# Light convolution and hard-swish feed-forward: block 0's exchange, last out bank and block 1's convolution put elsewhere in the order

## The chip, the cores and the metric

One core of one Trainium2 chip. The time is device microseconds of one execution of the program; the median of three runs is given. The engines are TensorE (PE, with its weight loads as PEld), VectorE (DVE), ScalarE (ACT), GpSimd (POOL), and SyncE (SP), which issues most DMAs.

## The reference

x is 8 sequences x 4096 tokens x 192 channels. The first part is a causal convolution of 7 taps, its weights a softmax for each of 8 groups of 24 channels; the second a feed-forward layer of width 2048 with a hard-swish gate. Cut to what matters:

```python
w = np.exp(weight - weight.max(-1, keepdims=True)); w = w / (w.sum(-1, keepdims=True) + 1e-9)
y[b, s, h, g] = sum(w[h, k] * x_pad[b, s + k, h, g] for k in range(7))      # 6 zeros ahead
h = y.reshape(32768, 192) @ w_in                                            # 192 x 2048
g = h * np.clip(h + 3.0, 0.0, 6.0) / 6.0
out = g @ w_out                                                             # 2048 x 192
```

x and the convolution's weight come as float32, w_in and w_out as 8-byte floats.

## The kernel before, in words

**Tiling.** 32768 tokens are 32 blocks of 1024, each two groups of 512. Channels lie on 64 partitions in three thirds; the lower 64 partitions hold one group of tokens, the upper 64 the other. `y` is the convolved block, [128, 3, 512]. It is split into a high part (ACT, L416) and a low part (DVE, L419), `y_own`, so that three passes of products (PASSES, L28) give the precision wanted. `y_other` is the same with the two halves of the partitions exchanged; the exchange is made by DMAs that SP issues (`swap`, L294 to L296).

**First layer.** A block has 16 units, each one of 8 pairs of columns of w_in for the own or the other half: 18 matmuls (L433) into one of four slots of two PSUM banks, then a relu on ACT (L307) and the gate on DVE (L311) into `g`. Slots go round in `free_slots`: a unit pops the first and appends it behind its gate.

**Second layer.** From block 1 on it is a scheme of products of sums (L503 on). Block 0 does it directly instead: `direct_chunk` (L356, matmuls at L322) adds one eighth of the sum into out banks, three banks in all. The first two are the two banks of one slot, `taken`, which is set aside at the unit r == 2; they are filled among the units of the loop and after it. The third is filled after that. `direct_out` transposes a bank on DVE (L367) and stores it.

**Start.** The weights' 8-byte words are loaded and rounded on the way, in 16 "units" of `Rounding` (L162): w_in 0, w_in 1, then w_in and w_out in turn, at last three of w_out. A load is 384 KB, two DMAs for w_in (L143) and one for w_out (L151), all issued by SP. `split` is two instructions of DVE (L181, L185), `clamp` three of ACT (L193, L196, L199), `join` two of DVE (L202, L206) and one of POOL (L210), `part`, for w_in alone, one of ACT (L218) and two of POOL (L219, L220). Four stages are there for w_out.

Inside `manual_schedule` (L716) every engine does its instructions in the order of the program. Block 0's convolution comes first, by thirds (`conv_units`, and for a third and a part PE itself, L731); as soon as a third of y is ready its parts are exchanged by `high_y` and `low_y`. The last third to come is number 1. `thirds_of` makes the first products of units 0 and 8 from the thirds that are there. Then the loop over r (L812) goes through the units, own and other in turn: products, relu, the `part` of the weight before, `clamp`, `join`, some loads, the gate, a `split`, and from r == 5 on every second time a chunk of the direct second layer. Behind the loop come `prepare` (block 1's convolution, one multiply on ACT and six taps on DVE, and the split of y), two last chunks, `direct_out` of the two banks, eight chunks of the third bank, `begin_block_two` (sums of w_out, small sums on POOL, part of block 2's convolution), `direct_out` of the third bank, the exchange for block 1, and the loop over blocks 1 to 31.

Of the kernel before, what the change touches and what calls it, by code (L numbers as in the profile page):

```python
# [8 lines left out]
ALU = mybir.AluOpType  # L9
# [22 lines left out]
def kernel(  # L32
# [8 lines left out]
    nc = tc.nc  # L41
# [3 lines left out]
    H, KC = weight.shape  # L45
# [3 lines left out]
    N = 512  # L49
# [43 lines left out]
    for base, dma in ((0, nc.scalar), (D2, nc.sync)):  # L93
        dma.dma_start(  # L94
            out=w_sb[base : base + D2],
# [4 lines left out]
    x_tiles = {0: xs.tile([P, K3, PAD + N], F32, name="x")}  # L100
    nc.vector.memset(x_tiles[0][0:D2, :, 0:PAD], 0.0)

    def load_x0(s, dma_lower, dma_upper):
        head, lower, upper = x_source(0)
        dma_lower.dma_start(out=x_tiles[0][0:D2, s, head:], in_=lower[:, s])  # L105
        dma_upper.dma_start(out=x_tiles[0][D2:P, s, :], in_=upper[:, s])
# [55 lines left out]
    class Rounding:  # L162
# [10 lines left out]
        def load(self):  # L173
            self.st = self.load_words()

        def split(self, engine=nc.vector):
            high = self.st[:, :, 1]
            self.top = cnv.tile([P, WS], U32, name="top")
            self.scale = cnv.tile([P, WS], U32, name="scale")
            self.sig = cnv.tile([P, WS], F32, name="sig")  # L180
            engine.tensor_scalar(  # L181
                out=self.scale[:], in0=high, scalar1=0x7FF00000, scalar2=None,
                op0=ALU.bitwise_and,
            )
            engine.tensor_scalar(  # L185
                out=self.top[:], in0=high, scalar1=0xFFFFF, scalar2=0x100000,
                op0=ALU.bitwise_and, op1=ALU.bitwise_or,
            )

        def clamp(self):  # L190


            nc.scalar.activation(  # L193
                self.sig[:], self.scale[:], ACT.Relu, bias=bias_e[:, 0:1], scale=-1.0
            )
            nc.scalar.activation(  # L196
                self.scale[:], self.sig[:], ACT.Relu, bias=bias_e[:, 1:2], scale=-8.0
            )
            nc.scalar.mul(self.sig[:], self.st[:, :, 0], 2.0**-52)  # L199

        def join(self):
            nc.vector.scalar_tensor_tensor(  # L202
                out=self.scale[:], in0=self.st[:, :, 1], scalar=0x80000000,
                in1=self.scale[:], op0=ALU.bitwise_and, op1=ALU.bitwise_or,
            )
            nc.vector.scalar_tensor_tensor(  # L206
                out=self.sig[:], in0=self.top[:], scalar=2.0**-20, in1=self.sig[:],
                op0=ALU.mult, op1=ALU.add,
            )
            nc.gpsimd.tensor_tensor(  # L210
                out=self.sig[:] if len(self.dst) > 1 else self.dst[0],
                in0=self.sig[:], in1=self.scale[:].bitcast(F32), op=ALU.mult,
            )

        def part(self):
            if len(self.dst) > 1:
                high, low, full = self.dst
                nc.scalar.mul(r32(high), self.sig[:], CUT)  # L218
                nc.gpsimd.tensor_copy(out=r32(full), in_=self.sig[:])  # L219
                nc.gpsimd.tensor_tensor(  # L220
                    out=r32(low), in0=self.sig[:], in1=high, op=ALU.subtract
                )
# [8 lines left out]
    def w_out_unit(j):  # L231
        dst = w_out[:, j, B11 : B22 + 1].rearrange("p b d -> p (b d)")
        return Rounding(lambda: load_w_out(j), [dst])
# [10 lines left out]
    for j in range(2, NP):  # L244
        units += [w_in_unit(j), w_out_unit(j - 2)]
    units += [w_out_unit(j) for j in range(NP - 2, NP)]
    AHEAD = 4
    for n in range(AHEAD):
        units[n].load()
        if n == 0:  # L250
            load_x0(1, nc.sync, nc.sync)
# [5 lines left out]
        out=e_sb[:], in0=w_sb[:], in1=mx[:].to_broadcast([P, KC]), op=ALU.subtract  # L257
# [3 lines left out]
    c_sb = cst.tile([P, KC], F32, name="c_sb")  # L261
# [5 lines left out]
    y = ys.tile([P, K3, N], F32, name="y")  # L267
# [35 lines left out]
    psum = ps.tile([P, 2 * 4, N], F32, name="psum")  # L303
    free_slots = list(range(4))

    def relu(r6, h):
        nc.scalar.activation(r6, h, ACT.Relu, bias=half[:], scale=1.0 / 6.0)  # L307

    def gate(g_, h):

        nc.vector.scalar_tensor_tensor(  # L311
            out=g_, in0=g_, scalar=1.0, in1=h, op0=ALU.min, op1=ALU.mult
        )
# [113 lines left out]
    def products(n, slot, s, steps=range(3), begin=False, end=False):  # L427
        group, c = divmod(n, NP)
        for m_ in steps:
            wn, yn = PASSES[m_]  # L430
            for k in range(2):
                r = slice(k * D2, (k + 1) * D2)
                nc.tensor.matmul(  # L433
                    out=psum[:, 2 * slot + k], lhsT=r32(w_in_parts[wn][r, c, s]),
                    rhs=r32(y_other[r, yn, s] if group else y_own[yn][r, s]),
                    start=begin and m_ == 0, stop=end and m_ == 2, skip_group_check=True,
                )

    def places(n, slot):
        group, c = divmod(n, NP)  # L440
        return g4[:, c, 1:3] if group else g4[:, c, 0::3], psum[:, 2 * slot : 2 * slot + 2]
# [274 lines left out]
    with tc.manual_schedule():  # L716
# [4 lines left out]
            out=c_sb[:], in0=e_sb[:], in1=sm[:].to_broadcast([P, KC]), op=ALU.mult  # L721
# [15 lines left out]
        for _ in range(3):  # L737

            nc.tensor.matmul(
                out=psum[:, b], lhsT=zeros[:, 0:P], rhs=zeros, start=True, stop=True  # L740
# [10 lines left out]
        def thirds_of(n, which, end=False):  # L751
            if n not in early:
                early[n] = free_slots.pop(0)
            for m_ in range(3):
                for s in which:
                    products(
                        n, early[n], s, (m_,), s == pe_third, end and s == which[-1]
                    )
# [5 lines left out]
        def low_y(s, of):  # L764
            low_of(y_own[LOW][:, thirds[s]], of, y_own[HIGH][:, thirds[s]], nc.vector)
            swap(y_other[:, LOW, thirds[s]], y_own[LOW][:, thirds[s]])

        def all_of(s):
            return y[:, thirds[s]]
# [14 lines left out]
        low_y(pe_third, psum[:, b : b + 1])  # L784
        high_y(0, all_of(0))
        low_y(0, all_of(0))
        for n in range(AHEAD, 2 * AHEAD):
            load(n)
        thirds_of(0, (pe_third, 0))
        thirds_of(NP, (pe_third, 0))  # L790
        split(1)
# [5 lines left out]
        join(1)  # L797
        part(1)
        low_y(1, all_of(1))
        for n in (8, 9, 10, 12):  # L800
            load(n)
        split(2)
        clamp(2)
# [1 line left out]
        thirds_of(0, (1,), True)  # L805
        thirds_of(NP, (1,), True)

        joins = {0: 2, **{n - 1: n for n in range(3, len(units))}}
        loads = {3: 11, 5: 13, 7: 14, 9: 15}
        taken = None  # L810
        waiting = [1]
        for r in range(2 * NP):  # L812
            c, group = divmod(r, 2)
            k = c + group * NP
            if k in early:
                slot = early[k]
            else:
                slot = free_slots.pop(0)
                for m_ in range(3):
                    for s in range(K3):  # L820
                        products(k, slot, s, (m_,), s == 0, s == K3 - 1)
            to, both = places(k, slot)
            relu(to, both)
            n = joins.get(r)
            if r - 1 in joins:
                part(joins[r - 1])
            if n is not None:
                clamp(n + 1)
                join(n)
                if n in loads:  # L830
                    load(loads[n])
            gate(to, both)
            if r == 2:
                taken = slot
                banks = [(h, psum[:, 2 * slot + h]) for h in range(2)]
                x_tiles[1] = load_x(1)
            else:
                free_slots.append(slot)
            if n is not None:
                split(n + 2)  # L840
            if r >= 5 and r % 2:
                direct_chunk(banks, (r - 5) // 2)
        start_pools.close()

        def conv_jobs(i):
            x = x_tiles.pop(i)
            jobs = [lambda: nc.scalar.mul(y[:], x[:, :, 0:N], c_sb[:, 0:1])]  # L847
            for k in range(1, KC):
                jobs.append(lambda k=k: nc.vector.scalar_tensor_tensor(  # L849
                    out=y[:], in0=x[:, :, k : k + N], scalar=c_sb[:, k : k + 1], in1=y[:],  # L850
                    op0=ALU.mult, op1=ALU.add,
                ))
            return jobs

        def split_y():
            split_high()
            split_rest()
# [5 lines left out]
            low_of(y_own[LOW][:], y[:], y_own[HIGH][:], nc.vector)  # L863

        def prepare():
            for job in conv_jobs(1):
                job()
            x_tiles[2] = load_x(2, nc.gpsimd)
            split_y()
# [14 lines left out]
        for r, bank in banks:  # L884
            direct_out(0, r, bank)
        free_slots.append(taken)
        third = 2, psum[:, 2 * free_slots[0]]
        for p in every:
            direct_chunk([third], p)
        begin_block_two()  # L890
# [7 lines left out]
        for i in range(1, NB):  # L898
            jobs = {4 * n + 1: [job] for n, job in enumerate(conv[4:])}
# [47 lines left out]
```

## Time and profile before

| | us |
|---|---|
| median of three runs | 2234.03 (2233.31 to 2237.73) |
| the profiled execution's own time | 2237.14 |
| its span | 2235.0 |
| PE busy | 2216.5 (99%) |
| DVE busy | 1811.7 (81%) |
| ACT busy | 936.0 (42%) |
| POOL busy | 829.0 (37%) |
| start to block 1's first product | 108.23 |
| block 1's first layer, second layer | 35.70, 35.47 |
| block 2's first layer, second layer | 32.87, 35.47 |

The profile is of one execution; L12 is line 12 of the kernel. Busy PE is modelled from pipelined matmuls, and says nothing of the clock that PE was granted, which is a row of its own (1.00 is full). A wait names the instruction that waited, what released it, and the time that its engine was idle. The span leaves out some 2 us of the execution's own time.

### The profile page before, as it was taken

How to read it: one execution, taken by the hardware profiler on the slowest of the kernel's cores; microseconds unless marked ns; L12 is line 12 of the kernel's file. 1: busy time of each engine (PE TensorE's matmuls, PEld its weight loads, DVE VectorE, ACT ScalarE, POOL GpSimd, SP SyncE). 2: the span in 40 equal slices, each digit the busy share in tenths (PEclk: the TensorE clock that was granted, in tenths of full speed). 3: DMA queues.
4: the chain of work that ended last, by engine and by line, in shares of the span. 5: the costliest groups of instructions: out<-in, count | busy, mean ns of one | idle time of the engine just before them, and what ended most of it. 6: DMA issues, size and time to landing. Idle time of an engine off the chain costs nothing.

```text
span 2235.0 us, 49342 instructions
## 1 busy us (share of the span) xinstructions
PE 2216.5 (99%) x21598; PEld 1543.1 (69%) x21598; DVE 1811.7 (81%) x1588; ACT 936.0 (42%) x1172; POOL 829.0 (37%) x706
## 2 busy tenths in 40 slices
PE   8999999999999999999999999999999999999999
PEld 4477766777766777667777667776677776677766
DVE  7878888888887888888888888888888888888866
ACT  6444433444333444334443334443344433344433
POOL 3344322444223443224442234432244422344322
PEclk9999999999999999999999999999999999999999
DMA  6143233342233332333322333223333223332232
GB/s 163 36 91 58 43 68 76 63 77 34 58 76 70 70 55 44 69 76 63 76 34 58 77 70 70 54 44 71 75 65 77 34 58 76 70 70 53 41 61 34
DMA packets 249096, 142.91 MB, mean 64 GB/s; under 512 B 207121, under 2 KB 212241, under 8 KB 248881
## 3 DMA queue, kind: packets, MB, share of 16 engines
q1 hardware_dynamic: 230392, 105.86, 23.4%
q0 software_dynamic: 17248, 33.64, 8.7%
q8 instruction: 169, 2.77, 0.5%
q10 hardware_dynamic: 1240, 0.27, 0.1%
q14 instruction: 47, 0.38, 0.1%
HBM read 31.72 MB, written 25.17 MB: 25 GB/s over the span
## 4 chain that ended last, share of the span: by engine, by line
PE 97%; DVE 1%; DMA 1%; SPq 0%; ACT 0%; issue 0%; POOL 0%; DVEq 0%; ACTq 0%; POOLq 0%
PE psum L529 49%; PE psum L433 47%; PE psum L322 1%; DVE y L849 1%; DMA x<-in_x_dram 0%; DMA y_other<-y 0%; SPq L143 0%; ACT y L847 0%; DVE y L284 0%; SPq L295 0%; SPq L105 0%; SPq L296 0%; SPq L151 0%; DVE results L401 0%; SPq L94 0%
## 5 line engine op out<-in xcount | busy, mean ns | idle before, releaser
L529 PE MATMUL psum<-g,w_out 128*32 128x512 f32 (+1 forms) x6712 | 967.4, 552 | 0.0
L311 DVE SCALAR_TENSOR_TENSOR g<-g,psum 128x1024 f32<-128x1024 f32 x512 | 618.9, 1218 | 213.4 <-ACT g L307 213.1
L307 ACT ACTIVATE g<-psum,half 128x1024 f32<-128x1024 f32 x512 | 572.4, 1118 | 506.2 <-PE psum L433 478.1
L492 POOL TENSOR_TENSOR s<-g 128x256 f32<-128x256 f32 x248 | 268.7, 1084 | 1252.1 <-DVE g L311 957.2
L433 PE MATMUL psum<-y,w_in 64*128 64x512 f32 x4608 | 538.5, 391 | 3.0 <-DVE results L367 3.0
L529 PEld LDWEIGHTS psum<-g,w_out 128*32 128x32 f32 x6712 | 370.9, 110 | 246.9 <-issue 126.7
L433 PE MATMUL psum<-y_other,w_in 64*128 64x512 f32 x4608 | 530.8, 387 | 8.4 <-DMA y_other<-y 8.1
L433 PEld LDWEIGHTS psum<-y,w_in 64*128 64x128 f32 x4608 | 434.1, 186 | 122.1 <-issue 29.8
L433 PEld LDWEIGHTS psum<-y_other,w_in 64*128 64x128 f32 x4608 | 434.2, 184 | 99.0 <-DMA y_other<-y 10.4
L529 PE MATMUL psum<-s,w_out 128*32 128x512 f32 (+1 forms) x3272 | 465.4, 570 | 0.0
L849 DVE SCALAR_TENSOR_TENSOR y<-x,c_sb,y 128x1536 f32<-128x1536 f32 x186 | 334.9, 1800 | 2.8 <-ACT y L847 1.6
L381 POOL TENSOR_TENSOR s<-g 128x1024 f32<-128x1024 f32 x93 | 297.8, 3202 | 25.1 <-DVE g L311 25.1
L529 PE MATMUL psum<-g,w_s 128*32 128x256 f32 x1240 | 282.8, 379 | 0.0
L529 PEld LDWEIGHTS psum<-s,w_out 128*32 128x32 f32 x3272 | 153.8, 110 | 80.1 <-issue 48.4
L529 PEld LDWEIGHTS psum<-g,w_s 128*32 128x32 f32 x1240 | 136.4, 110 | 68.2
L381 DVE TENSOR_TENSOR s<-g 128x2048 f32<-128x2048 f32 (+1 forms) x93 | 177.2, 1934 | 1.1
L529 PE MATMUL psum<-s,w_s 128*32 128x256 f32 x744 | 170.7, 379 | 0.0
L492 DVE TENSOR_TENSOR g<-g 128x1024 f32<-128x1024 f32 x124 | 151.9, 1225 | 5.3
L381 DVE TENSOR_TENSOR g<-g 128x2048 f32<-128x2048 f32 x62 | 139.1, 2284 | 0.0
L401 DVE TENSOR_TENSOR p<-psum,p 32x256 f32<-32x256 f32 (+1 forms) x93 | 47.7, 513 | 96.5 <-PE psum L529 95.1
L401 DVE TENSOR_TENSOR results<-psum,results 32x256 f32<-32x256 f32 (+3 forms) x128 | 69.2, 541 | 51.0 <-issue 47.2
L526 ACT COPY psum<-psum 32x512 f32<-32x512 f32 x93 | 51.3, 551 | 135.4 <-PE psum L529 135.4
(88 smaller groups left out, 1092.1 us busy)
## 6 DMA issues: line engine op xcount, KB each, us to landing
y_other<-y SPq DMA_DIRECT2D x124, 384.0 KB, 5.0
g<-g POOLq DMA_DIRECT2D x62, 512.0 KB, 5.0
out_dram<-results SPq DMA_DIRECT2D x378, 64.0 KB, 2.0
x<-in_x_dram SPq DMA_DIRECT2D x53, 388.5 KB, 7.1
g<-in_moe_w_in_dram SPq DMA_DIRECT2D x16, 192.0 KB, 5.6
stage<-in_moe_w_out_dram SPq DMA_DIRECT2D x8, 384.0 KB, 3.9
x<-in_x_dram SPq DMA_DIRECT2D x7, 384.0 KB, 6.5
y_other<-y SPq DMA_DIRECT2D x12, 128.0 KB, 2.3
```

The source lines that it names most:

```text
L307: nc.scalar.activation(r6, h, ACT.Relu, bias=half[:], scale=1.0 / 6.0)
L311: nc.vector.scalar_tensor_tensor(out=g_, in0=g_, scalar=1.0, in1=h, op0=ALU.min, op1=ALU.mult)
L322: lambda p=p: nc.tensor.matmul(out=bank[j * QS : (j + 1) * QS, tokens], lhsT=w_out[:, p, w, cols], rhs=x[:, p, tokens], start=(first and p ...
L381: engine.tensor_tensor(out=o[:, r], in0=a[:, r], in1=b[:, r], op=op)
L401: nc.vector.tensor_tensor(out=out, in0=x, in1=y, op=op)
L433: nc.tensor.matmul(out=psum[:, 2 * slot + k], lhsT=r32(w_in_parts[wn][r, c, s]), rhs=r32(y_other[r, yn, s] if group else y_own[yn][r, s]), ...
L492: engine.tensor_tensor(out=o, in0=p, in1=q, op=op)
L526: streams[3].append((t - 0.5, lambda: fn(*args, **kw)))
L529: nc.tensor.matmul(out=out, lhsT=w, rhs=x, start=start, stop=True, tile_position=(0, j * QS), skip_group_check=True,)
L849: jobs.append(lambda k=k: nc.vector.scalar_tensor_tensor(out=y[:], in0=x[:, :, k : k + N], scalar=c_sb[:, k : k + 1], in1=y[:], op0=ALU.mu ...
```

## The change

It has three parts, all of them in block 0 or just behind it; the arithmetic is the same.

1. Three weight units instead of four are loaded at the start. Unit 3 is loaded behind the exchange of third 0, where units 4 to 7 were, and these are loaded behind the exchange of third 1, ahead of 8, 9, 10 and 12.
2. Block 1's convolution is taken apart: its multiply on ACT is issued at the end of r == 6 of the loop, one tap at the ends of r == 9, 11, 13 and 14, and the last two taps where all seven instructions were, in `prepare`.
3. The third out bank is a bank of the last slot in `free_slots`, not of the first.

```diff
-    AHEAD = 4
-    for n in range(AHEAD):
+    for n in range(3):
         units[n].load()
...
         low_y(0, all_of(0))
-        for n in range(AHEAD, 2 * AHEAD):
-            load(n)
+        load(3)
         thirds_of(0, (pe_third, 0))
         thirds_of(NP, (pe_third, 0))
...
         low_y(1, all_of(1))
-        for n in (8, 9, 10, 12):
+        for n in (4, 5, 6, 7, 8, 9, 10, 12):
             load(n)
...
+        conv1 = []
         joins = {0: 2, **{n - 1: n for n in range(3, len(units))}}
...
             if n is not None:
                 split(n + 2)
+            if r == 6:
+                conv1.extend(conv_jobs(1))
+                conv1.pop(0)()
+            if r in (9, 11, 13, 14):
+                conv1.pop(0)()
             if r >= 5 and r % 2:
                 direct_chunk(banks, (r - 5) // 2)
...
         def prepare():
-            for job in conv_jobs(1):
+            for job in conv1:
                 job()
             x_tiles[2] = load_x(2, nc.gpsimd)
             split_y()
...
         free_slots.append(taken)
-        third = 2, psum[:, 2 * free_slots[0]]
+        third = 2, psum[:, 2 * free_slots[-1]]
         for p in every:
             direct_chunk([third], p)
```

`conv_jobs` itself only moves ahead of the loop: it returns the multiply (L847) and the six taps (L849) as a list.

More of the change, by code (lines that the diff above doesn't have):

```diff
@@ L806, with conv_jobs @@
         thirds_of(NP, (1,), True)
+        def conv_jobs(i):
+            x = x_tiles.pop(i)
+            jobs = [lambda: nc.scalar.mul(y[:], x[:, :, 0:N], c_sb[:, 0:1])]
+            for k in range(1, KC):
+                jobs.append(lambda k=k: nc.vector.scalar_tensor_tensor(
+                    out=y[:], in0=x[:, :, k : k + N], scalar=c_sb[:, k : k + 1], in1=y[:],
+                    op0=ALU.mult, op1=ALU.add,
+                ))
+            return jobs
+        conv1 = []
         joins = {0: 2, **{n - 1: n for n in range(3, len(units))}}
@@ L843 @@
         start_pools.close()
[L845 to L853, printed above, removed]
         def split_y():
```

## The prediction

> **What bounds the kernel.** I read the page first, its chain that ended last:
>
> ```profile
> PE 97%; DVE 1%; DMA 1%; SPq 0%; ACT 0%; issue 0%; POOL 0%; DVEq 0%; ACTq 0%; POOLq 0%
> ```
>
> TensorE (PE) has 97% of the span, so only idle or slowed PE time is worth anything. Next all waits of PE (us in total, times, longest):
>
> ```profile
> PE psum L433 <- DMA y_other<-y: 8.1, 2, 7.3
> PE psum L433 <- DVE results L367: 3.0, 1, 3.0
> ```
>
> Besides 1.7 us at the very start that is all PE waits in 2235 us. Where they lie is in PE's timeline (start, duration, instruction, count, idle before), 16 to 46 us and behind 91 us:
>
> ```profile
> 21.04 0.85 PE L433 MATMUL psum<-y,w_in 64*128 64x512 f32 x6
> 29.20 2.16 PE L433 MATMUL psum<-y_other,w_in 64*128 64x512 f32 x6 [7.32 <-DMA y_other<-y]
> 31.16 4.04 PE L433 MATMUL psum<-y,w_in 64*128 64x512 f32 x18
> ...
> 107.38 0.71 DVE L367 STREAM_TRANSPOSE results<-psum 128x512 f32<-128x512 f32 x1
> ...
> 108.23 19.38 PE L433 MATMUL psum<-y,w_in 64*128 64x512 f32 x144 [3.04 <-DVE results L367]
> ```
>
> Both lie at block 0. The first product that needs the exchanged last third of y waits 7.32 us; block 1's first product waits 3.04 us until the third out bank is transposed out of the slot it takes first. Each wait costs more than itself. In the table of stages (columns: PE, PEld, DVE, ACT, POOL busy, granted clock, DMA share, GB/s)
>
> ```profile
> 18.53:21.95 3.42, 2.42 (x18) 1.34 (x16) 3.42 (x5) 1.61 (x4) 2.80 (x3) 1.00 0.84 219
> 103.87:107.28 3.41, 1.32 (x16) 0.13 (x4) 3.38 (x2) 0.00 (x0) 0.00 (x0) 1.00 0.09 13
> 107.28:110.69 3.41, 2.46 (x12) 2.16 (x14) 3.37 (x4) 0.00 (x0) 0.00 (x0) 0.50 0.38 61
> ```
>
> the granted clock falls to 0.50 at 107.3 us and is back at 114.1; around the other wait it is 0.50 from 25.4 to 35.6. 18 matmuls take 4.04 us at 31.16, and 2.2 at full clock. Block 1's first layer lasts 108.23 to 143.93 = 35.70 us, block 2's 32.87: 2.83 us of slow clock.
>
> Why the exchange is late is in SP's queue:
>
> ```profile
> 18.30 0.60 SPq L296 DMA_DIRECT2D y_other<-y  x1
> 18.94 1.25 SPq L143 DMA_DIRECT2D g<-in_moe_w_in_dram  x2
> 20.24 0.60 SPq L151 DMA_DIRECT2D stage<-in_moe_w_out_dram  x1
> 20.88 1.18 SPq L143 DMA_DIRECT2D g<-in_moe_w_in_dram  x2
> 22.11 0.59 SPq L151 DMA_DIRECT2D stage<-in_moe_w_out_dram  x1
> 22.80 0.50 SPq L295 DMA_DIRECT2D y_other<-y  x1
> ```
>
> y's last third was ready (L416, L419) at 18.68 and 19.55, but units 4 to 7 (6 DMAs, 4 x 384 KB = 1.57 MB) are issued first, and at some 240 GB/s they take 6.5 us. The exchange then lands 6 us after issue, against 2.2 at best.
>
> **Part 1, the loads.** Unit 3 (one DMA, 0.6 us of SP) moves from 7.67 to 18.94; units 4 to 7 (3.9 us of SP) go behind the exchange. The exchange is issued at 19.54, 20.1 (high), 20.7, 21.3 (low), ending 21.9. Ahead of it in the queue is unit 3 alone (1.6 us at 240 GB/s, to 21.8). Bounds for landing: with nothing ahead 2.3 us behind issue, 22.4 and 23.6; with unit 3 and 0.55 us for each 128 KB behind one another, 22.9 and 24.0. I take 22.7 and 23.9; unit (r=) 2 of the loop starts at 24.2 instead of 31.16. PE is idle 0.8 + 0.65 us; the stretch 18.53:21.95 had 1.0 us idle and held the clock. If it fell here, that is 1.7 us, mostly taken up below, where DVE decides.
>
> What is late next? Unit 3 lands at about 22, so its split (L181, L185) is done at 22.75 and the first gate still starts at 23.76 as before. Unit 4 is issued at 22.0 and lands behind the exchange at 24.0 + 1.6 = 25.6 to 26; DVE waits 1.0 us for it. All loads to unit 12 then are landed at 24.0 + 8 x 1.6 = 36.8, unit 11 at 38.4, x of block 1 (0.78 MB) at 41.7; needed at 42.6 (below). The weight of r=6 is ready on POOL (L220) at 35.5; PE is there at 36.4 and reads that part 0.7 later. 1.6 us of slack, no wait.
>
> PE: 24.2 + 2 pairs of 4.30 + a chunk of 3.57 = 36.4 for r=6 (before 45.11, of which 2 us was slow clock); five pairs with chunk of 7.87 and two chunks of 3.57 later the two out banks are full at 82.9 (before 91.6).
>
> **Part 2, the convolution of block 1.** Before, ACT L847 (1.57 us) and six taps L849 (1.83 each) came behind all gates. Now the multiply stands behind r=6, four taps behind r=9, 11, 13, 14, two after. No work is added; what counts is DVE's queue. Its stretch in the table of stages:
>
> ```profile
> 23.76:98.08 74.32, 68.73 (x578) 35.71 (x582) 56.85 (x74) 43.34 (x62) 27.79 (x29) 0.93 0.30 73
> ```
>
> and DVE's waits, 20 to 100 us:
>
> ```profile
> DVE g L311 <- ACT g L307: 15.7, 9, 6.9
> DVE y L419 <- ACT y L416: 1.6, 1, 1.6
> ```
>
> From the first gate (23.76) to the end of block 1's low part (98.08) DVE worked 56.85 of 74.32 us and waited 15.7 for gates' relus, which wait for PE. The same instructions now have waits of 1.6 (high part on ACT), 1.0 (unit 4), some 0.6 (relu of r=1): 23.76 + 56.85 + 3.2 = 83.8. A pair of gates with splits and joins costs DVE 6.6 of PE's 7.87 us; with a tap 8.4, so DVE falls behind 0.6 a pair, which the three gates of slot rotation (a gate may be 2 to 5 us late) and weights that are ready 2 to 3 us early hold. On ACT 1.57 fits the 1.84 us that ACT idles per pair. POOL works slower beside a tap: L492 at 117.83 takes 2.25 us beside a tap begun at 117.67, later ones 0.75; 1.5 us, within the same slack.
>
> The Trainium skill, page "SBUF — State Buffer", section "SBUF: two separate sides", says that the port pair of VectorE and GpSimd is an exclusive lock and the loser waits out the whole instruction. The trace agrees (L492 above; L181 is 0.35 us or 1.17 beside POOL). The rule speaks against packing taps among splits; it is the slower rival below.
>
> **Part 3, the slot.** `free_slots[-1]` is the slot `taken`, just appended: its bank 0 is one of the two out banks. So the third bank's matmuls (128 records, 91.66 to 105.19 = 13.55 us) now wait for the first transpose (0.65 us) instead of running at once; block 1's first product waits for nothing. Its fourth unit takes that slot 6.1 us later; the transpose behind it (DVE free since about 94) needs 0.7. Bounds of the added wait: the transpose alone, 0.05 + 0.65 + 0.14 (L367's end 108.09 to PE 108.23) = 0.84 us, if DVE is there at 82.9; DVE at 83.8 gives 83.8 + 0.65 + 0.14 = 84.6, PE idle 1.75. I take the latter. Block 1's own exchange is issued some 2.8 us after that transpose, by 106, lands by 111; needed at 98.2 + 8 x 2.04 = 114.5.
>
> **Sum.** 84.65 + 13.55 = 98.2 for block 1's first product, before 108.23: 10.0 us; and 2.83 of slow clock in block 1: 12.9. Of that the profiled execution's own time is 2237.14 (span 2235.0 and 2.14 around it): 2224.3. The median of the runs shown is 3.1 lower; two of four runs lie near 2237.5, two near 2233.7, about the half of two clock stretches apart (2 x 1.7), so I hold it for luck with the slow clock that now goes, and don't take it off. If it lies elsewhere, 2221.2.
>
> **Rivals.**
> 1. *Clock falls at the third bank.* 1.32 us busy in 3.41 lost the clock, 2.42 kept it; 1.75 idle leaves 1.66 if one stretch holds it all. Then one stretch at half: 1.7 us, 2226.0. The Trainium skill, "TensorE: Matmul & The Clock Gate", section "What's actually happening", has the clock fall after a whole idle window of about 3.4 us that runs freely; by that it would hold. The stretch at 103.87, 39% busy, disagrees, so the row decides.
> 2. *DVE is later still* by 2 to 3 us (x of block 1 lands behind 42.6, holding ACT's queue; or splits lengthen), clock falls: 2224.3 + 2.5 + 1.7 = 2228.5. The slack of x is 0.9 us.
> 3. *DVE is on time*: 0.84 wait only: 2223.4.
> 4. *The exchange isn't sooner* (landing set by something other than what is ahead in the queue): banks full at 91.6, third bank at 92.45, block 1 at 106.0: 2.2 + 2.83, 2232.1. Against it: its siblings with nothing ahead landed in 2.3 us.
> 5. *Slower: splits against POOL.* The 24 split instructions from the first gate on take 14.75 us (mean 0.61), between 0.35 and 1.18 by what POOL does beside them. All at 1.18 are 28.3: DVE at 97.4, third bank at 98.2, block 1 at 111.8, clock lost as before: 2237.14 + 3.5 = 2240.7. Slower than before from 10 of these 13.6 us on. Against it: the splits' neighbours on POOL are the same ones.
>
> **Chances.** Forecast 0.42, rival 1 0.30, rival 2 0.10, rival 3 0.07, rival 4 0.06, rival 5 0.05. A measurement of this kernel can tell 0.2% (4.5 us). Faster by over that (under 2229.6): 0.42 + 0.30 + 0.10 + 0.07 less 0.01 = 0.88; same 0.07; slower 0.05. The range goes from rival 3 with the median's 3.1 off, 2220.3, to rival 2 and a little, 2229.0; outside are rivals 4 and 5.
>
> **What would show it.** Right: PE's wait for y_other in two pieces under 1 us, clock 1.00 to 80 us; r=6's product near 36; taps among L311 with no PE wait; PE's one wait for L367 at L322 instead of L433, 1 to 2.5 us; block 1's first layer 32.9 us. Wrong: a wait of PE for POOL L220 or for L311 between 36 and 83; ACT L847 waiting for x; third bank begun behind 87.

## The result, and the profile after

| | before | after |
|---|---|---|
| median, us | 2234.17 (2233.31 to 2237.73) | 2226.05 (2224.83 to 2226.84) |
| the profiled execution's own time, us | 2237.14 | 2225.98 |
| its span, us | 2235.0 | 2223.9 |
| first product of loop unit r=2 / r=6, us | 31.16 / 45.11 | 25.91 / 39.34 |
| block 1's first product, us | 108.23 | 99.94 |
| block 1's first layer, us | 35.70 | 32.88 |

The ratio is 0.9959, 95% interval 0.9946 to 0.9972: faster by 0.4%. By medians that is 8.1 us. Between the two profiled executions 108.23 - 99.94 = 8.29 us come from block 1 starting earlier and 35.70 - 32.88 = 2.82 from its first layer at full clock. That is 11.1 of the 11.16 us between them, so nothing changed behind block 1's first layer. They lie further apart than the medians because before's profiled execution is 3.0 us above its median; the changed kernel's is at its own. (The changed kernel has one line less ahead of these: L432 is L433 of before, L366 is L367, L321 is L322, L310 is L311; the taps are at L810.)

The chain that ended last, on the page of the changed kernel, still is PE:

```profile
PE 98%; DVE 1%; DMA 0%; ACT 0%; SPq 0%; issue 0%; POOLq 0%; DVEq 0%; ACTq 0%
```

All waits of PE in the changed kernel (total, times, longest):

```profile
PE psum L432 <- DMA y_other<-y: 3.7, 3, 2.4
PE psum L738 <- DVE half L262: 1.5, 1, 1.5
PE psum L321 <- DVE results L366: 0.4, 1, 0.4
```

The 1.5 us are at the very start, as before. The exchange's 8.1 us became 3.7. The wait for the transpose moved from block 1's first product (L433 of before) to the third out bank (L321) and shrank from 3.0 to 0.4. PE's timeline shows where they lie:

```profile
24.46 0.73 PE L432 MATMUL psum<-y_other,w_in 64*128 64x512 f32 x4 [2.38 <-DMA y_other<-y]
25.54 0.58 PE L432 MATMUL psum<-y_other,w_in 64*128 64x512 f32 x2 [0.34 <-DMA y_other<-y]
25.91 3.78 PE L432 MATMUL psum<-y,w_in 64*128 64x512 f32 x18
...
86.06 13.94 PE L321 MATMUL psum<-g,w_out 128*32 128x512 f32 x128 [0.38 <-DVE results L366]
99.94 16.64 PE L432 MATMUL psum<-y,w_in 64*128 64x512 f32 x144
```

Block 1 starts at 99.94 with no wait in front of it. But 18 matmuls at 25.91 still take 3.78 us instead of 2.2, so the clock was low there. The table of stages, in stretches of 3.41 us, the clock's own steps (PE, PEld, DVE, ACT, POOL busy, granted clock, DMA share, GB/s; a clock of 0.99 or 0.51 is a stretch that lies across a step by some hundredths of a us):

```profile
22.46:25.87 3.41, 1.06 (x6) 0.60 (x8) 2.18 (x5) 3.18 (x5) 0.53 (x1) 0.99 1.04 243
25.87:29.29 3.42, 3.42 (x18) 2.66 (x16) 2.52 (x5) 1.60 (x3) 1.98 (x3) 0.51 1.08 264
83.89:87.30 3.41, 3.03 (x32) 0.71 (x28) 3.41 (x4) 0.00 (x0) 3.31 (x5) 1.00 0.88 208
```

After the exchange one stretch ran at half clock, that is at 0.50 (before, three), at the third bank none. SP's queue around the exchange:

```profile
19.16 0.59 SPq L151 DMA_DIRECT2D stage<-in_moe_w_out_dram  x1
19.84 0.47 SPq L294 DMA_DIRECT2D y_other<-y  x1
...
22.27 1.26 SPq L143 DMA_DIRECT2D g<-in_moe_w_in_dram  x2
```

Only unit 3 (L151) is left in front of it. The four DMAs of the exchange are out by 22.2, ahead of units 4 to 7. Last, DVE: its stretch from the first gate on in the table of stages,

```profile
25.17:85.00 59.83, 59.49 (x508) 32.90 (x510) 54.82 (x74) 42.38 (x61) 26.48 (x29) 0.97 0.39 92
```

and its waits, 20 to 100 us:

```profile
DVE g L310 <- ACT g L306: 2.3, 3, 0.9
DVE scale L181 <- DMA stage<-in_moe_w_out_dram: 2.3, 1, 2.3
DVE y L418 <- ACT y L415: 1.6, 1, 1.6
...
DVE scale L181 <- DMA g<-in_moe_w_in_dram: 0.9, 1, 0.9
```

DVE worked 54.8 of 59.8 us; the gates' waits for relus fell from 15.7 us to 2.3. A new wait stands there, 2.3 us for unit 3's words (`stage`). It lies ahead of the first gate, which therefore starts at 25.17 instead of 23.76, as DVE's timeline shows (with the two out banks' transposes at its end):

```profile
23.69 0.36 DVE L181 TENSOR_SCALAR scale<-stage 128x384 uint32<-128x384 uint32 x1 [2.27 <-DMA stage<-in_moe_w_out_dram]
...
25.17 1.21 DVE L310 SCALAR_TENSOR_TENSOR g<-g,psum 128x1024 f32<-128x1024 f32 x1
...
85.30 1.31 DVE L366 STREAM_TRANSPOSE results<-psum 128x512 f32<-128x512 f32 x2
```

### The profile page after: what moved, and what is told of

It is laid out like the page before. It is cut to its first block, busy times and chain, and to the rows that moved or that the text cites. A ratio compares the mean times of both kernels' runs of the same rounds, so it can differ in the third digit from the quotient of the medians.

```text
span 2223.9 us, 49341 instructions
## 1 busy us (share of the span) xinstructions
PE 2212.9 (100%) x21598; PEld 1537.5 (69%) x21598; DVE 1809.7 (81%) x1588; ACT 935.4 (42%) x1172; POOL 827.1 (37%) x706
## 3 DMA queue, kind: packets, MB, share of 16 engines
HBM read 31.72 MB, written 25.17 MB: 26 GB/s over the span
## 4 chain that ended last, share of the span: by engine, by line
PE 98%; DVE 1%; DMA 0%; ACT 0%; SPq 0%; issue 0%; POOLq 0%; DVEq 0%; ACTq 0%
PE psum L528 49%; PE psum L432 47%; PE psum L321 1%; DVE y L810 0%; DMA x<-in_x_dram 0%; DMA y_other<-y 0%; DVE y L418 0%; DVE y L283 0%; DVE g L310 0%; ACT y L415 0%; DVE scale L181 0%; SPq L105 0%; SPq L143 0%; ACT g L306 0%; DVE top L185 0%
## 5 line engine op out<-in xcount | busy, mean ns | idle before, releaser
L310 DVE SCALAR_TENSOR_TENSOR g<-g,psum 128x1024 f32<-128x1024 f32 x512 | 618.9, 1218 | 196.3 <-ACT g L306 195.8
L432 PE MATMUL psum<-y,w_in 64*128 64x512 f32 x4608 | 535.5, 389 | 0.0
L432 PE MATMUL psum<-y_other,w_in 64*128 64x512 f32 x4608 | 529.8, 386 | 3.9 <-DMA y_other<-y 3.7
L432 PEld LDWEIGHTS psum<-y,w_in 64*128 64x128 f32 x4608 | 430.3, 185 | 119.9 <-issue 26.7
L432 PEld LDWEIGHTS psum<-y_other,w_in 64*128 64x128 f32 x4608 | 431.9, 184 | 95.7 <-DMA y_other<-y 5.6
L810 DVE SCALAR_TENSOR_TENSOR y<-x,c_sb,y 128x1536 f32<-128x1536 f32 x186 | 335.1, 1802 | 2.3 <-ACT y L808 1.2
```

The costliest lines, as they stand in the source:

```text
L310: nc.vector.scalar_tensor_tensor(out=g_, in0=g_, scalar=1.0, in1=h, op0=ALU.min, op1=ALU.mult)
L432: nc.tensor.matmul(out=psum[:, 2 * slot + k], lhsT=r32(w_in_parts[wn][r, c, s]), rhs=r32(y_other[r, yn, s] if group else y_own[yn][r, s]), ...
L810: jobs.append(lambda k=k: nc.vector.scalar_tensor_tensor(out=y[:], in0=x[:, :, k : k + N], scalar=c_sb[:, k : k + 1], in1=y[:], op0=ALU.mu ...
```

## The experiments

Each was timed in five rounds beside the kernel before on the same chip; ratios are to that kernel, whose median was 2233.97 to 2234.61 us there. My theory was that of the prediction: the loads decide when PE gets through block 0, DVE decides at the out banks, and the third bank's slot decides which of PE's matmuls waits for DVE. The main rivals: that DVE decides throughout, so that the loads bring nothing, and that one part does it all.

### The parts alone

Part 1 alone is the kernel before with the first three hunks of the diff.

> The kernel before with part 1 alone (loads behind the exchange). Theory (loads bring PE forward, DVE then decides at block 1): unit r=2 starts near 25.9 and the two out banks are full near 85.7 as in the changed kernel; the third bank runs at once to 99.3, but DVE has all six taps behind the gates, transposes the third bank near 101.6, and block 1's first product waits some 2.4 us, after which the clock falls for a stretch or two: 2229.5. Rival (the loads bring everything by themselves, DVE has room): no wait at block 1, 2226. Second rival (DVE decides from start to end, so an earlier exchange brings nothing): 2234.

Measured: 2228.79 us, ratio 0.9976 (0.9967 to 0.9985). Waits of PE:

```profile
PE psum L432 <- DVE results L366: 3.0, 1, 3.0
PE psum L432 <- DMA y_other<-y: 2.5, 2, 1.9
```

The theory's wait is there, at block 1's first product (102.97 us), and both rivals fall. PE was through the third bank 5.2 us earlier than before (100.0, 105.2); DVE, with six taps in one piece behind the gates, held block 1 up for 3.0.

The changed kernel without part 1:

> The changed kernel with part 1 undone (loads as before, parts 2 and 3 kept). Theory: out banks full near 91.6 as before, third bank's wait under 1 us, block 1's first product near 106 without slow clock behind it: 2229 to 2232, by how long the clock stays slow at the start. Rival (DVE decides, loads bring nothing): 2226, as the changed kernel.

Measured: 2230.99 us, 0.9984 (0.9975 to 0.9993). PE waits 0.4 us at the third bank, block 1's first product is at 106.23, and its first layer has full clock. As the theory had it; DVE does not decide on its own.

Part 3 alone is one line:

```diff
-        third = 2, psum[:, 2 * free_slots[0]]
+        third = 2, psum[:, 2 * free_slots[-1]]
```

> The kernel before with part 3 alone (third out bank in the slot set aside). Theory: the third bank waits for the first transpose, which DVE does at 98.0 behind all taps: PE idle from 91.7 to 98.8, 7 us, and a slow clock behind it; block 1's first product near 115 without a wait: 2237 to 2239, slower than before. Rival (the slot alone cures the wait of 3.04 us and the slow clock behind it): 2229.

Measured: 2241.30 us, 1.0031 (1.0019 to 1.0042), slower than before. Waits of PE:

```profile
PE psum L433 <- DMA y_other<-y: 8.3, 3, 7.6
PE psum L322 <- DVE results L367: 7.3, 1, 7.3
```

The slot alone is harmful: 3.0 us at block 1 turn into 7.3 at the third bank, with 6.8 us of half clock around its end. That is 2 us more than I expected at most.

Part 2 alone:

> The kernel before with part 2 alone (block 1's convolution among the gates, loads and slot as before). Theory: DVE is done with block 1's y near 90.5, so the third bank's transpose follows PE at once and block 1's first product waits 0.8 us instead of 3.04, clock kept: 2229 to 2232, the same as with part 3 beside it. Rival (the taps only shift DVE's work, the slot is what cures): 2234.

Measured: 2231.32 us, 0.9986 (0.9977 to 0.9994), the same as parts 2 and 3 together within the intervals. Its wait at block 1's first product is

```profile
PE psum L433 <- DVE results L367: 0.9, 1, 0.9
```

So of the two, part 2 is what cures; part 3 trades 0.9 us in one place for 0.4 in another, and only because part 2 has emptied DVE's queue. By medians: part 1 alone -5.8 us, part 2 -3.3, part 3 +6.7, 2 and 3 together -3.6, all three -8.1. Parts 1 and 2 with the slot of before were not run, so what part 3 adds beside them is open.

### Unit 3, and the slot

The changed kernel has unit 3 between the exchanges of thirds 0 and 1. Here it is back at the start:

```diff
-    for n in range(3):
+    for n in range(4):
         units[n].load()
...
-        load(3)
```

> The changed kernel, but with unit 3 loaded at the start again (units 4 to 7 stay behind the exchange). Theory (unit 3 ahead of the exchange costs its landing 1.6 us, and DVE waits 2.3 us for unit 3): the exchange lands at 22.6 and 23.8 instead of 24.5 and 25.5, DVE's wait for unit 3 is gone, first gate near 23.9, and DVE, which then decides, is at the out banks near 83.9: 1.3 to 1.5 us less than the changed kernel, 2224.6. Rival (the landing is set by the four exchange DMAs themselves): 2226, unchanged.

Measured: 2224.24 us, 0.9959 (0.9945 to 0.9972). The ratio is that of the changed kernel, so the 1.8 us between the medians are not clear of noise; what unit 3 does is read from the trace. PE's timeline:

```profile
22.04 0.74 PE L432 MATMUL psum<-y_other,w_in 64*128 64x512 f32 x4
23.34 0.50 PE L432 MATMUL psum<-y_other,w_in 64*128 64x512 f32 x2 [0.56 <-DMA y_other<-y]
...
83.66 13.94 PE L321 MATMUL psum<-g,w_out 128*32 128x512 f32 x128 [1.78 <-DVE results L366]
97.53 16.61 PE L432 MATMUL psum<-y,w_in 64*128 64x512 f32 x144
```

The high part is there with no wait at 22.04 and the low part at 23.34, 2.4 and 2.2 us ahead of the changed kernel. The first gate starts at 23.84, the third bank waits 1.78 us for DVE, and block 1 starts at 97.53 instead of 99.94: the rival falls. Third bank and median are close to what I had forecast for the change itself (1.75 us, 2224.3).

Next, the third bank in a slot that is neither the out banks' nor the one block 1 takes first:

```diff
-        third = 2, psum[:, 2 * free_slots[-1]]
+        third = 2, psum[:, 2 * free_slots[2]]
```

> The changed kernel with the third out bank in the third slot of the four (neither the slot of the two full out banks nor the one that block 1 takes first). Theory: no wait at the third bank and none at block 1; the 0.4 us at the third bank go and nothing else, as PE and DVE arrived there together: 2225.6. Rival (DVE alone decided, PE had room): 1 us or more less, 2225 or below.

Measured: 2224.58 us, 0.9956 (0.9944 to 0.9969). The wait is gone. 1.0 us more than expected went with it, and the time lies where the rival had it (2225 or below). In the profiled execution the exchange happened to leave no half clock (below). The loop's r=6 was at 37.26, and from there to full out banks PE takes 46.3 us in the traces above; so the banks were full near 83.6, an estimate, while DVE transposed them only from 85.44 on:

```profile
85.44 1.31 DVE L366 STREAM_TRANSPOSE results<-psum 128x512 f32<-128x512 f32 x2
```

With the slot of the change PE would have waited some 2.6 us there, by the same estimate. So the rival looks right for an execution that keeps its clock: PE then has room, and DVE alone decides in the changed kernel. How much of the median is the slot's stays open.

Both edits together:

> Both of the two edits: unit 3 loaded at the start, third out bank in the third slot. Theory (with the slot DVE no longer decides, so the whole of PE's earlier start counts): block 1's first product near 96.7 instead of 99.9, 2222.8. Rival (the two edits' gains are the same gain): 2224.6, as with unit 3 alone.

Measured: 2221.62 us, 0.9943 (0.9931 to 0.9956), the five runs within 0.3 us. All of PE's waits for the exchange are

```profile
PE psum L432 <- DMA y_other<-y: 1.5, 2, 0.8
```

and there is none for a transpose; block 1's first product is at 95.45. The gains are not the same gain: with DVE out of the way, PE's earlier start counts in full. This version beats both kernels: by medians it is 4.4 us under the changed one, and its slowest run (2221.70) is below the fastest of that (2224.83).

And is part 2 needed then? The loads and the third slot, convolution in one piece as before:

> The kernel before with part 1 and the third out bank in the third slot; block 1's convolution stays in one piece behind the gates (part 2 left out). Theory (the convolution among the gates is needed only where PE waits for a transpose that stands behind it in DVE's queue): DVE transposes the third bank near 102.5, block 1's third unit takes that slot near 104, so no wait: 2225.6, as with part 2. Rival (DVE's late end holds block 1 up in some other place): 2228.8, as with part 1 alone.

Measured: 2224.16 us, 0.9956 (0.9944 to 0.9969), the same as with part 2, though 1.4 under what I expected. With unit 3 early as well:

> Unit 3 early and the third out bank in the third slot, but block 1's convolution left in one piece behind the gates (part 2 left out). Theory (part 2 is needed only for the slot that the change chose): DVE transposes the third bank near 99, block 1's third unit takes that slot at 99.6: no wait, 2221.6, the same as with part 2. Rival (PE is now so early that DVE's queue holds up block 1's third unit): a wait of 1 to 2 us there, 2223 to 2225.

Measured: 2221.59 us, 0.9941 (0.9928 to 0.9954), the same as with part 2 again. DVE transposes the third bank 2 us behind PE,

```profile
97.71 0.71 DVE L366 STREAM_TRANSPOSE results<-psum 128x512 f32<-128x512 f32 x1
```

and nobody waits, since block 1 takes that slot only with its third unit. Rival refuted: part 2 pays only for the slots in which a matmul stands directly behind the transpose.

Unit 3 the other way, behind the exchange too:

```diff
-        load(3)
...
-        for n in (4, 5, 6, 7, 8, 9, 10, 12):
+        for n in (3, 4, 5, 6, 7, 8, 9, 10, 12):
```

> The changed kernel with unit 3 behind the exchange too, first of the loads there. Theory (unit 3 costs twice: what is ahead of the exchange delays PE, and unit 3's own landing delays DVE's first gate): the exchange lands as with unit 3 early (22.0 and 23.3), but unit 3 only near 25.5, so the first gate starts near 27, 2 us later than in the changed kernel, and DVE, which decides at the out banks, is there near 87.3: the third bank waits some 4 us, a stretch of slow clock with it: 2228 to 2230. Rival (PE's earlier start is what counts, DVE catches up): 2224.2, as with unit 3 early.

Measured: 2226.36 us, 0.9965 (0.9953 to 0.9978), the same as the changed kernel. Waits of PE:

```profile
PE psum L321 <- DVE results L366: 1.9, 1, 1.9
...
PE psum L432 <- POOL w_in L220: 1.0, 2, 0.7
PE psum L432 <- ACT w_in L218: 0.9, 1, 0.9
```

The mechanism is the theory's, the size is not. The exchange lands at 22.0 and 23.35 us, DVE waits 3.6 us for unit 3 and the first gate starts at 26.61. PE then waits 1.9 us for rounded weights, which I had not counted, and 1.9 instead of 4 at the third bank, with no half clock: it comes there later itself (84.6), and DVE earlier (near 85.7 instead of 87.3; 59.1 us from the first gate). Neither the 2228 to 2230 that I expected nor the rival's 2224.2 came, though one of the six runs took 2230.95 us, at a mean clock of 0.998 against 0.999 or 1.000 in the others. By the traces, block 1's first product comes 2.4 us later with unit 3 between the exchanges, and 2.8 us later with it behind them, than with an early load.

## Why the prediction was right, and where it was off

**Forecast 2224.3, measured 2226.05.** The mechanism and the sign held. Of 12.9 us that the sum gave, 11.1 came between the profiled executions. Block 1's first product came at 99.94 instead of 98.2; the step that cost most of these 1.7 us is the start of DVE's stretch.

**Part 1, first gate: mis-sized.** I had unit 3 landed "at about 22" and the first gate at 23.76 "as before". It landed near 23.7, and the first gate moved to 25.17. DVE was at the out banks at 85.30 instead of 83.8, and the third bank began at 86.06 instead of 84.65. From there to block 1 took 13.88 us, where I had 13.55. These 1.4 and 0.3 are the 1.7 us. With unit 3 early, the first gate at 23.84, the third bank began at 83.66.

**Part 1, landing of the exchange: mis-sized too.** I took 22.7 and 23.9 us, with unit 3 ahead of it taking 1.6 us of the queue at 240 GB/s. Measured are 24.46 and 25.54, outside my bounds of 22.9 and 24.0. Without unit 3 there it is at most 22.04, and 23.34. In the four traces with unit 3 between the exchanges the high part lands at 23.80 to 24.46, in the four without by 21.95 to 22.08. Some 0.6 us of it is SP's time to issue unit 3 (at 19.16), which I had counted. The rest is the time of the exchange's own DMAs from issue to landing: in each of those four traces the slowest took 3.5 to 4.1 us, without unit 3 there 2.4; I had allowed 2.6.

**The clock at the start.** I counted 0.8 + 0.65 us idle and held the clock. It was 2.38 + 0.34, and one stretch at half followed; r=2 of the loop took 1.6 us longer. That and the landing put r=6 at 39.34 instead of 36.4 and the full out banks at 85.7 instead of 82.9.

**Part 2: right, its 60 us in part by luck.** DVE needed 60.1 us from the first gate to the transposes; I had 23.76 to 83.8, 60.0. But the work in it was 55.1 us, not 56.85, and the waits 5.0, not 3.2: two errors that cancel. The gates waited 2.3 us for relus, where I had 0.6; 0.9 of it is the gate at 47.56, whose relu stood on ACT behind block 1's multiply (44.95 to 46.5), which I had taken to fit in for nothing. No wait of PE for weights or gates came up. The taps took 1.80 to 2.05 us, the longest (56.13) beside POOL's L219, itself 0.88 us long instead of 0.5 to 0.6. By the Trainium skill's "SBUF — State Buffer", section "SBUF: two separate sides", the engine that starts first holds the port pair they share for its whole instruction, and the other blocks. Here both instructions were longer, so this place shows that the two hold each other up, by 0.25 us for the tap, but does not bear out that rule. Rival 5 did not come: the 24 split instructions took 13.8 us, not 14.75 and far from 28.3.

**Part 3: the wait is there, but 0.38 us instead of 1.75.** PE came 2.8 us later than I had it and DVE 1.5 us, so both arrived nearly together. That they did is luck: PE's 2.8 us went into that wait and cost nothing more, DVE's 1.5 came through to block 1.

**Rivals.** The number of rival 1 (2226.0) is the measured one, but by chance: the clock fell behind the exchange and not at the third bank, and what it cost there was taken up by the wait for DVE. Rival 4 is refuted by part 1 alone (-5.8 us). The slack of x for block 1 sufficed: the multiply started at 44.95 with no wait for x.

**The median.** I kept the 3.1 us by which before's profiled execution lay above its median as luck with the slow clock. Before's six runs beside the changed kernel do lie in two groups, around 2234 and 2237.7. Its 46 runs beside the experiments do not; they are spread from 2232.9 to 2238.4. The ten of them with a mean clock of 0.996 or less have a median of 2237.0, the others 2233.9, so the longer runs are in the main those with more half clock. The changed kernel's runs lie between 2224.8 and 2226.8, and the five of the version with both edits within 0.3 us. That fits, but where each run lost the clock is not on record, so it is argued, not shown.

## What to carry to other kernels

A wait does not vanish by moving the buffer it is on: ask which instruction takes that buffer next and what stands ahead of its release in the other engine's queue. Of the three slots tried, the best was neither waiting for a transpose itself nor the first that block 1 takes, and with it a reordered convolution was not needed at all. A load directly ahead of a short, urgent transfer costs it the load's issue as well as its bytes; a load that could go earlier, into an idle queue, should. And after shortening one engine's path, see where the other arrives: here both came within 0.4 us, and neither the early load nor the other slot alone gave what the two gave together.

## What the runs showed of the hardware

The granted clock has only the values 1.00 and 0.50 and changes in steps of 3.41 us whose phase differs from run to run. It fell behind stretches in which PE was busy about half or less, not idle. In the traces of all twelve kernels, around the waits, it fell behind 0, 30, 33, 38, 42, 46 and 48% busy, and held behind 55, 58, 61, 63 and all more. Close to the border are, part 1 with the third slot (`loads_slot2`):

```profile
20.31:23.73 3.42, 1.59 (x12) 0.67 (x8) 1.88 (x5) 3.04 (x5) 1.83 (x3) 1.00 0.94 266
23.73:27.14 3.41, 3.34 (x14) 2.27 (x16) 2.21 (x5) 3.14 (x6) 1.51 (x2) 0.50 1.04 270
```

unit 3 early (`unit3_early`):

```profile
79.99:83.41 3.42, 1.88 (x20) 0.37 (x12) 2.19 (x2) 1.20 (x1) 3.08 (x4) 1.00 0.42 116
83.41:86.82 3.41, 3.17 (x32) 1.07 (x36) 3.34 (x5) 0.00 (x0) 3.33 (x5) 1.00 1.04 192
```

1.59 us busy lost the clock for the next stretch, 1.88 kept it. It came back only behind a stretch at half clock that was 98% busy or more: 73, 80, 84 and 91% were not enough. A gap of about 2 us therefore costs a stretch at half clock, some 1.7 us by its length, or nothing, by where it falls in the steps: the loads with the third slot lost the clock behind a wait of 1.74 us, the changed kernel with the third slot kept it behind 1.91 and 0.37. The Trainium skill, "TensorE: Matmul & The Clock Gate", section "What's actually happening", has the clock fall after a whole idle window; these runs do not agree with that, while its free-running window of about 3.4 us they bear out.
